# Six ring slots, leftovers loaded ahead by ScalarE, and the mask added on TensorE in a segment-recurrent attention kernel

## The chip, the cores and the metric

The kernel runs on one core of a Trainium2 chip. The metric is device time in microseconds of one execution. Four runs of the kernel before gave a median of 2346.21 us (2343.95 to 2352.86); the profiled execution took 2343.33 us.

## The reference

Two attentions run over 2048 rows of width 640, and their outputs are put side by side. The first, A, is a sliding, dilated attention with 32 heads of 20. The second, B, is a recurrence, and most of the time lies there:

```python
for s in range(64):                                  # 2048 rows in segments of 32
    h = concat([mem, x[32*s : 32*s+32]])             # 8 memory rows + 32 rows = 40
    q, k, v = h @ Wq, h @ Wk, h @ Wv                 # 32 heads of 192: 640 -> 6144, each
    p = softmax(where(mask, q @ k.T * scale, -1e9))  # 40 x 40 per head
    o = (p @ v) @ Wo                                 # 6144 -> 640
    mem, out = o[:8], o[8:]
```

The memory of a segment is the first 8 rows of the output of the one before, so the segments cannot be done side by side. The mask lets every row see the memory, memory rows see all, and the others see what is not later than themselves.

## The kernel before, in words

**Part A** (0 to 236 us of the span) computes the first attention; `between` (line 404) slips work for B into it. **The left phase** (236 to 461 us) does ahead, for all segments at once, what does not depend on the memory: of the 32 rows of a segment the last 8, the "leftovers", have their queries, keys and values computed and put into HBM (`qk_scr`, `v_scr`). The other 24 rows go with the 8 memory rows as one block of 32 columns through **the segment loop** (461 to 2262 us, 64 iterations). **The tail** (2262 to 2341 us) multiplies the leftovers' results, which the loop has put into `ol_scr`, by Wo for all segments.

One iteration projects the 32 columns with twelve weight groups, Q0, K0, Q1, K1 to Q3, K3 and V0 to V3, each of 8 heads (`proj`, line 583: 20 matmuls of 128x32 by 384 columns, four side by side). ACT copies the Q results and DVE the K results to bf16 in one of three buffers `abc0` to `abc2` (`keep_`, line 598), PE transposes Q and K of a group (`turn`), ACT and DVE copy the turned heads into `XL` (`turned_out`, line 616). `scores(0)` uses groups 0 and 1, `scores(1)` groups 2 and 3; the softmax of each half runs on DVE and ACT in three pieces (`softmax_1` to `softmax_3`); `turn_p` transposes the probabilities, `pv` multiplies by V, `heads_out` and `left_out` copy the results, and sixteen output units (`o_units`, 12 matmuls each) sum Wo's part into one bank. Two DVE steps then make the next segment's input `HT` from it.

**The weights.** They do not all fit in SBUF. Of every projection group the heads of j = 0, 1, 2 stay resident, and the unit of j = 3 (128 rows of 1,920 bf16, 480 KB) is streamed in each iteration; so are four of the sixteen output units, 16 streamed units in all. They take turns in five ring slots (four in `temp`, one in `ring4`). `SLOT` (line 365) says which unit sits where, and `done` (line 571) issues, on SyncE, the load of the unit that follows in a slot as soon as the matmuls that used the slot are through:

```python
SLOT = [0, 1, 2, 3, 0, 4, 1, 2, 0, 3, 4, 1, 0, 2, 3, 4]  # Q0 K0 Q1 K1 Q2 K2 Q3 K3 V0 V1 V2 V3 and four output units
```

**The order.** Each engine runs its own list in the order in which lines 747 to 808 call. `SegmentLoop.analyse` (line 240) works out the semaphore waits from named resources that an operation reads and writes. An operation can name resources as `also`: it waits for their readers, and counts as a reader of them itself. DMAs are operations of the engine that issues them, and a wait ahead of one holds everything behind it on that engine. SyncE's list holds the weight loads, the leftovers' queries and keys (`load_left`, line 623, two in an iteration), their values (`load_vl`) and four loads of the next segment's rows (line 755). `load_left` puts queries and keys side by side over memory that `OT` and `PT` share, and POOL copies the queries into place (line 625). ACT's list holds, beside its copies, the store of the leftovers' results (line 801) and of the output rows (line 808).

## Time and profile before

| what | value |
|---|---|
| median of 4 runs | 2346.21 us |
| profiled execution | 2343.33 us, its span 2341.2 us |
| busy in the span | PE 75%, weight loads on PE 48%, DVE 41%, ACT 30%, POOL 2% |
| granted TensorE clock | 0.943 |
| HBM read, written | 573.62 MB, 39.62 MB |
| DMA engines | 261 GB/s over the span |

In the profile a row of a group has line, engine, operation, out<-in, shapes and count, then busy us and mean ns of one, then idle us of the engine just before and what ended that. A row of a wait has who waited for whom: total us, times, longest us. A row of the order in time has start us, us, engine, line, operation, and in brackets the idle time before it. "SPq" and "ACTq" are the DMA issues of SyncE and ACT. The DMA share is the mean over the core's 16 DMA engines.

### The profile page before, as it was taken

What the parts mean: (1) busy time and instruction counts of PE and PEld (TensorE: products, weight loads), DVE (VectorE), ACT (ScalarE), POOL (GpSimd) and SP (SyncE); (2) the same over time, 40 slices, a digit from 0 to 9 for tenths busy, and PEclk for the clock granted to TensorE, in tenths of its full rate; (3) what the DMA queues carried; (4) which work ended last, traced back from release to release, by engine and by line L of the source; (5) the groups of instructions that cost most, each with busy time, mean ns of one, the idle gap of its engine ahead of it and who ended that gap; (6) DMA issues with size and microseconds to landing.
All of it is one profiled execution on the core that took longest, in us unless ns stands there. A gap on an engine that the chain in (4) does not pass through costs nothing.

```text
span 2341.2 us, 108094 instructions
## 1 busy us (share of the span) xinstructions
PE 1765.8 (75%) x45924; PEld 1113.1 (48%) x45948; DVE 961.2 (41%) x2284; ACT 691.8 (30%) x1633; POOL 50.5 (2%) x150
## 2 busy tenths in 40 slices
PE   7796958777777777777787777777777777777749
PEld 5442423355445554554455545454454444444436
DVE  3575312244444444444444444444444444444430
ACT  4342312123323333222332333222222323222221
POOL 0000000000000000000000000000000000000000
PEclk9898979799999999899999999999989999999989
DMA  8030975789888888888998889888888888888881
GB/s 225 22 105 20 188 225 178 230 281 317 297 291 307 301 304 302 288 291 292 311 305 293 299 296 310 292 292 304 301 283 290 292 289 301 286 293 284 287 311 62
DMA packets 259558, 611.24 MB, mean 261 GB/s; under 512 B 90608, under 2 KB 120432, under 8 KB 256768
## 3 DMA queue, kind: packets, MB, share of 16 engines
q1 hardware_dynamic: 223872, 591.35, 75.7%
q10 hardware_dynamic: 35648, 19.34, 2.8%
q8 instruction: 29, 0.48, 0.1%
q14 instruction: 9, 0.07, 0.0%
HBM read 573.62 MB, written 39.62 MB: 262 GB/s over the span
## 4 chain that ended last, share of the span: by engine, by line
issue 76%; PE 12%; DMA 6%; DVE 2%; ACT 1%; POOL 1%; POOLq 0%; ACTq 0%; SPq 0%; DVEq 0%
PE pq L75 3%; PE ps L444 3%; PE yp L836 2%; DMA v_scr<-abc 2%; DMA temp<-in_B_Wk_dram 1%; DMA ws<-temp 1%; DVE pv L157 1%; PE po L87 1%; PE ps L458 1%; POOL XL L625 1%; PE oT L162 1%; DMA temp<-in_B_Wo_dram 1%; DMA v_scr<-ring 1%; PE L L108 1%; PE pp L141 0%
## 5 line engine op out<-in xcount | busy, mean ns | idle before, releaser
L592 PE MATMUL bank<-temp,XL 128*32 128x384 bf16 x3200 | 641.8, 339 | 0.0
L592 PE MATMUL bank<-w,XL 128*32 128x384 bf16 x7680 | 530.2, 346 | 62.8 <-DMA temp<-ws 62.4
L592 PE MATMUL bank<-wq,XL 128*32 128x384 bf16 x3840 | 265.6, 339 | 217.7 <-DMA temp<-ws 201.2
L600 ACT CAST abc<-bank 128x384 bf16<-128x384 f32 x512 | 240.3, 479 | 577.3 <-PE bank L592 571.5
L592 PEld LDWEIGHTS bank<-w,XL 128*32 128x32 bf16 x7680 | 243.6, 100 | 233.6 <-DMA temp<-ws 85.7
L592 PEld LDWEIGHTS bank<-temp,XL 128*32 128x32 bf16 x3200 | 279.3, 99 | 0.0
L592 PEld LDWEIGHTS bank<-wq,XL 128*32 128x32 bf16 x3840 | 114.0, 98 | 323.1 <-DMA temp<-ws 262.1
L618 DVE COPY XL<-bank 128x384 bf16<-128x384 bf16 x256 | 90.9, 355 | 353.5 <-PE bank L612 203.3
L739 PE MATMUL bank<-w,XL 128*32 128x160 bf16 x9216 | 231.5, 236 | 1.5 <-issue 1.5
L600 DVE CAST abc<-bank 128x384 bf16<-128x384 f32 x256 | 141.6, 553 | 205.0 <-PE bank L592 204.9
L651 PE MATMUL bank<-XL 128*64 128x40 bf16 (+1 forms) x4096 | 123.2, 189 | 110.4 <-POOL XL L625 110.3
L739 PEld LDWEIGHTS bank<-w,XL 128*32 128x32 bf16 x9216 | 173.5, 98 | 19.8 <-issue 3.7
L618 ACT COPY XL<-bank 128x384 bf16<-128x384 bf16 x256 | 122.7, 479 | 191.9 <-PE bank L612 109.2
L651 PEld LDWEIGHTS bank<-XL 128*64 128x64 bf16 (+1 forms) x4096 | 106.1, 112 | 151.5 <-POOL XL L625 144.9
L721 ACT CAST XL<-bank 128x192 bf16<-128x192 f32 x256 | 81.7, 319 | 232.0 <-PE bank L714 155.2
L721 DVE CAST XL<-bank 128x192 bf16<-128x192 f32 x256 | 91.0, 355 | 138.7 <-ACT XL L721 138.6
L592 PE MATMUL bank<-ring,XL 128*32 128x384 bf16 x640 | 145.6, 365 | 0.0
L612 PE MATMUL bank<-ident,abc 128*128 128x128 bf16 x1536 | 136.3, 227 | 0.1
L612 PEld LDWEIGHTS bank<-ident,abc 128*128 128x128 bf16 x1536 | 90.6, 101 | 86.9 <-issue 45.7
L662 DVE SCALAR_TENSOR_TENSOR t<-bank,XL 128x320 f32<-128x320 f32 x128 | 62.9, 492 | 122.9 <-PE bank L651 122.9
L625 POOL COPY XL<-XL 128x192 bf16<-128x192 bf16 x128 | 44.7, 349 | 1752.1 <-DMA XL<-qk_scr 1752.1
L688 PE MATMUL bank<-ident,t 128*128 128x128 bf16 x256 | 36.7, 225 | 55.5 <-DVE t L679 55.5
(111 smaller groups left out, 2039.8 us busy)
## 6 DMA issues: line engine op xcount, KB each, us to landing
temp<-ws SPq DMA_DIRECT2D x644, 480.0 KB, 5.1
temp<-in_B_Wo_dram SPq DMA_DIRECT2D x196, 480.0 KB, 5.3
ring<-ws SPq DMA_DIRECT2D x129, 480.0 KB, 6.1
ring<-in_B_Wo_dram SPq DMA_DIRECT2D x64, 480.0 KB, 3.4
qk_scr<-st SPq DMA_DIRECT2D x2, 6144.0 KB, 17.3
XL<-qk_scr SPq DMA_DIRECT2D x128, 96.0 KB, 4.3
abc<-v_scr SPq DMA_DIRECT2D x64, 96.0 KB, 4.3
ol_scr<-XL ACTq DMA_DIRECT2D x64, 96.0 KB, 6.7
```

The source lines that it names most:

```text
L75: nc.tensor.matmul(pq[32 * dd:32 * dd + 32, :], lhsT=w[:, 4 * c + dd, :], rhs=xT[:, dc, :], start=(dc == 0), stop=(dc == 4), tile_position ...
L444: nc.tensor.matmul(ps[:], lhsT=w[:, dc, o:o + 128], rhs=XL[:, dc], start=(dc == 0), stop=(dc == 4))
L592: i = MM(ps[32 * j:32 * j + 32, :], lhsT=HT[:, dc, :], rhs=ws[j][:, dc, :], start=(dc == 0), stop=(dc == 4), tile_position=(0, 32 * j))
L600: op(e, [f"b{b}"], [f"abc{k}"], lambda s: COPY[e](ABC[k], bank[b][:, 0:384]))
L612: i = nc.tensor.transpose(tp[ty][:, c], ABC[nat[ty, r]][:, 128 * c:128 * c + 128], ident)
L618: op(e, [("b3", "b5")[ty]], [QPARTS[ty][h]], lambda s: COPY[e](QT[:, 12 * h:12 * h + 12, 0:32] if ty == Q else KT[:, 12 * h:12 * h + 12, 0:4],
L625: op("POOL", ["PT", "PTL"], ["Q.l"], lambda s: nc.gpsimd.tensor_copy(QT[:, :, 32:L], ql))
L651: i = MM(Sps[64 * e:64 * e + 64, 4 * rr + j, :], lhsT=XLb[lo:hi, L * (4 * cc + j):L * (4 * cc + j) + 64], rhs=KT[lo:hi, 4 * cc + j], start ...
L662: op("DVE", [f"b{SB[t]}"], ["t1"], lambda s: V_.scalar_tensor_tensor(out=t1[:], in0=Sps, scalar=scale, in1=mask.unsqueeze(1).to_broadcast( ...
L721: op(e, [f"b{4 + j}"], [f"OT{t}.{j}"], lambda s: COPY[e](OT[t][:, 6 * j:6 * j + 6], ots[j].rearrange("p r x l -> p (r x) l")[:, :, 0:32]), ...
L739: i = MM(Y[32 * g:32 * g + 32], lhsT=OT[t][:, 6 * j + 3 * rr + x], rhs=w[:, x, 160 * g:160 * g + 160], start=(t == 0 and n == 0 and x == 0 ...
L836: nc.tensor.matmul(yp[h][:], lhsT=OL[tb][:, 24 * (r // 2) + 6 * j + 3 * (r % 2) + x].rearrange("p s l -> p (s l)"), rhs=w[:, x, 320 * h:32 ...
```

## The change

- **Ring.** Six slots and 17 streamed units: output units (1,0), (0,3), (2,0), (2,2), (3,3) are streamed instead of (0,2), (0,3), (2,1), (2,3), so 11 output units stay resident instead of 12. `SLOT` is new. The tail loads five units instead of four.
- **Queues.** SyncE's list in the loop holds weight loads only. The leftovers' keys, queries, values and the next rows are loaded by ACT. Keys and queries are loaded separately; those of half 0 are loaded in the iteration before, through one more row of `qk_scr`. The next rows come as one load of 128 rows, for which `x_scr` has another layout, with zeros where the memory rows stand; it is written by 12 transfers in part A.
- **Waits.** An operation that names a resource as `also` no longer waits for others that do; only a writer waits for both. The results of the two halves lie elsewhere (`OT`, `OL`), and the leftovers' store is split in two.
- **Softmax.** The mask, divided by the scale, is added in PSUM by two matmuls with the identity ahead of each score block; the scale is applied in the exponential. The DVE pass that scaled and masked is gone, and the next two read PSUM.
- **Order.** Q3 is copied after turn 2 and into another buffer; five output units (not three) stand ahead of the second `turn_p`, and three (not two) behind it; none of the first half stands behind the second `pv`.
- **Rows in HBM.** The streamed units' scratch has rows of 2,048 elements of which 1,920 are used.

SyncE's list at the start of an iteration of the kernel before; `ws_0_2_3` is Q's (0) group 2, unit j = 3, `ws_1` is K's, `ws_2` V's:

```order
L575 DMA temp_88<-ws_0_2_3_72 128x1920
L575 DMA temp_88<-ws_0_3_3_74 128x1920
L575 DMA temp_88<-ws_1_3_3_75 128x1920
L624 DMA XL_89<-qk_scr_81 128x2x192
L575 DMA temp_88<-ws_2_1_3_77 128x1920
L756 DMA z_3577<-x_scr_80 24x160
L575 DMA temp_88<-ws_2_0_3_76 128x1920
```

The row of z stands four times there. The same place in the changed kernel, issued after Q0, K0, Q1, K1, Q2 and K2 have used their slots:

```order
L584 DMA temp_87<-ws_0_3_3_73 128x1920
L584 DMA temp_87<-ws_2_0_3_75 128x1920
L584 DMA temp_87<-ws_1_3_3_74 128x1920
L584 DMA temp_87<-ws_2_1_3_76 128x1920
L584 DMA ring4_3587<-ws_2_2_3_77 128x1920
L584 DMA ring5_3588<-in_B_Wo_dram 128x1920
```

Q0's slot now takes Q3's unit and not Q2's, and nothing but weights is left in the list.

ACT's list before, from the first copy of turned probabilities to the exponential of the second half (a register row is the count of a wait):

```order
L692 COPY XL<-bank_4000 128x160
L325 REGISTER_ALU
L721 CAST XL<-bank_4001 128x192
L325 REGISTER_ALU
L721 CAST XL<-bank_4001 128x192
L670 ACTIVATE t_2613<-t_2613 128x320
```

The same place in the changed kernel, from the load of the next rows on:

```order
L796 DMA z<-x_scr 128x160
L330 REGISTER_ALU
L705 COPY XL<-bank_4010 128x160
L330 REGISTER_ALU
L734 CAST XL<-bank_4011 128x192 x2
L330 REGISTER_ALU
L683 ACTIVATE t_2624<-t_2624 128x320
```

The two copies of heads follow each other without a wait between, and a DMA issue has come ahead of them.

ACT's list before, at the end of an iteration:

```order
L692 COPY XL<-bank_4000 128x160
L721 CAST XL<-bank_4001 128x192
L801 DMA ol_scr<-XL 128x2x192
L807 ACTIVATE z<-bank_3999,bdf 128x160
L808 DMA out_dram<-z 4x32x160
```

And in the changed kernel, from the copy of V3 on:

```order
L609 CAST abc_2622<-bank_4008 128x384
L743 DMA ol_scr<-XL 128x192
L633 DMA XL<-qk_scr 128x192
L705 COPY XL<-bank_4010 128x160
L734 CAST XL<-bank_4011 128x192 x2
L636 DMA XL<-qk_scr 128x192
L743 DMA ol_scr<-t_2624 128x192
L825 CAST z<-bank_4009 128x160
L826 DMA out_dram<-z 4x32x160
```

The first store (L743) and the loads of the next iteration's keys (L633) and queries (L636) now stand among the copies.

The diff, cut to its core:

```diff
-                for k in rd + also:
+                for k in rd:
                     readers.setdefault(k, []).append(me)
+                for k in also:
+                    takers.setdefault(k, []).append(me)
...
-    N_STR, N_RING = 16, 5
-    SLOT = [0, 1, 2, 3, 0, 4, 1, 2, 0, 3, 4, 1, 0, 2, 3, 4]
+    N_STR, N_RING = 17, 6
+    SLOT = [0, 1, 2, 3, 4, 5, 0, 2, 1, 3, 4, 0, 1, 2, 3, 4, 5]
...
-    ws_scr = {u: dram.tile([128, US], BF16, name=f"ws_{u[0]}_{u[1]}_{u[2]}") for u in streamed if u[0] != O}
+    ws_scr = {u: dram.tile([128, 2048], BF16, name=f"ws_{u[0]}_{u[1]}_{u[2]}")[:, 0:US] for u in streamed if u[0] != O}
...
-    OT = [XLb[:, KO * t:KO * t + 4 * PW].rearrange("p (a l) -> p a l", l=32) for t in range(2)]
-    OL = XLb[:, 0:2 * KO].rearrange("p (t n) -> p t n", t=2)[:, :, 4 * PW:5 * PW]
+    OT = [XLb[:, o:o + 4 * PW].rearrange("p (a l) -> p a l", l=32) for o in (KO, 0)]
+    OL = [XLb[:, 4 * PW:KO], t1b[:, 256:256 + PW]]
...
-    def load_left(t):
-        op("SP", [], ["K.l", "PT", "PTL"], lambda s: nc.sync.dma_start(left, qk_scr[:, :, t, s, :]), dma="qkl")
-        op("POOL", ["PT", "PTL"], ["Q.l"], lambda s: nc.gpsimd.tensor_copy(QT[:, :, 32:L], ql))
+    def load_kl(t, ahead):
+        op("ACT", [], ["K.l"], lambda s: nc.scalar.dma_start(kl, qk_scr[:, 0, t, s + ahead, :]), dma="kl")
+    def load_ql(t, ahead):
+        op("ACT", [], ["PT", "PTL"], lambda s: nc.scalar.dma_start(ql, qk_scr[:, 1, t, s + ahead, :]), dma="ql")
+    def place_ql():
+        op("POOL", ["PT", "PTL"], ["Q.l", "Q.e"], lambda s: nc.gpsimd.tensor_copy(QT[:, :, 32:L], ql.rearrange("p (a k) -> p a k", k=NL)))
     def load_vl():
-        op("SP", [], ["abc2"], lambda s: nc.sync.dma_start(ABC[2], v_scr[s]), dma="vl")
+        op("ACT", [], ["abc2"], lambda s: nc.scalar.dma_start(ABC[2], v_scr[s]), dma="vl")
...
+            for e in range(2):
+                h = slice(64 * e, 64 * e + 64)
+                MM(Sps[h], lhsT=ident[h, h], rhs=mask[h].unsqueeze(1).to_broadcast([64, 8, L]), start=True, stop=False,
+                   tile_position=(64 * e, 64 * e), skip_group_check=True)
...
-        op("DVE", [f"b{SB[t]}"], ["t1"], lambda s: V_.scalar_tensor_tensor(
-            out=t1[:], in0=Sps, scalar=scale, in1=mask.unsqueeze(1).to_broadcast([128, 8, L]),
-            op0=ALU.mult, op1=ALU.add))
-        op("DVE", ["t1"], ["mx"], lambda s: V_.tensor_reduce(out=mx, in_=t1[:], axis=AX.X, op=ALU.max))
+        op("DVE", [f"b{SB[t]}"], ["mx"], lambda s: V_.tensor_reduce(out=mx, in_=Sps, axis=AX.X, op=ALU.max))
...
-    load_left(0)
     turn(0)
...
     qk(K, 1)
-    for g in range(4):
-        op("SP", [], [ZG[g]], lambda s, g=g: nc.sync.dma_start(
-            z[32 * g:32 * g + NX, :], x_scr[s + 1, 0:NX, 160 * g:160 * g + 160]), dma="xz")
+    load_ql(1, 0)
...
+    load_vl()
     qk(K, 2)
     scores(0)
+    load_kl(1, 0)
+    place_ql()
     softmax_1(0)
-    qk(Q, 3)
-    load_left(1)
+    proj(Q, 3)
     turn(2)
+    keep_("ACT", Q, 3)
...
+    store_left(0)
+    load_kl(0, 1)
     softmax_3(1)
-    o_units(0, 0, 3)
+    o_units(0, 0, 5)
     turn_p(1)
-    o_units(0, 3, 5)
+    o_units(0, 5, 8)
     pv(1)
...
-    o_units(0, 5, 8)
+    load_ql(0, 1)
+    store_left(1)
     o_units(1, 0, 8)
```

More of the change, by code (lines that the diff above doesn't have):

```diff
@@ L268, in analyse @@
                         want(ev, True)
+                    if k in wr:
+                        for ev in takers.get(k, []):
+                            want(ev, True)
                     if k in writer:
@@ L362, in part_b @@
         order += [(O, 2 * t + rr, j) for j in range(4) for rr in range(2)]
-    streamed = [u for u in order if u[0] != O and u[2] == 3 or u in ((O, 0, 2), (O, 0, 3), (O, 2, 1), (O, 2, 3))]
-    N_STR, N_RING = 16, 5
-    SLOT = [0, 1, 2, 3, 0, 4, 1, 2, 0, 3, 4, 1, 0, 2, 3, 4]
+    streamed = [u for u in order if u[0] != O and u[2] == 3 or u in ((O, 1, 0), (O, 0, 3), (O, 2, 0), (O, 2, 2), (O, 3, 3))]
+    N_STR, N_RING = 17, 6
+    SLOT = [0, 1, 2, 3, 4, 5, 0, 2, 1, 3, 4, 0, 1, 2, 3, 4, 5]
     assert len(streamed) == N_STR
@@ L502, in part_b @@
     psum = lctx.enter_context(tc.tile_pool(name="b_ps", bufs=1, space=PSUM))
-    rows, toks = bdf[:, 3:4], bdf[:, 4:5]
+    rows = bdf[:, 3:4]
     XLb = XL[:].rearrange("p c s l -> p (c s l)")
@@ L742, in emit @@
                 return i
[L743 removed]
+            op("PE", [f"OT{t}.{j}", wkey(u)] + OPARTS[t], ["b2"], emit)
             done([u])
[L746 removed]
     qk(Q, 0)
+    place_ql()
     qk(K, 0)
     qk(Q, 1)
[L750 removed]
     turn(0)
@@ L780, in part_b @@
     keep_("ACT", V, 1)
+    op("ACT", [], ["z"], lambda s: nc.scalar.dma_start(z[:], x_scr[s + 1]), dma="xz")
     turn_p(0)
```

89 lines of the change are left out of this document (45 added, 44 removed).

## The prediction

> **What bounds the kernel now.** I read the page first, then stretches by stage, the waits, the queue of SyncE, and one iteration in order of time. The page gives the span; the stretches are part A, the left phase, the segment loop and the tail.
>
> ```profile
> span 2341.2 us, 108094 instructions
> ...
> 0.00:236.00 236.00, 183.27 (x1870) 99.50 (x1885) 133.58 (x99) 86.27 (x152) 4.34 (x14) 0.91 0.34 92
> 236.00:461.00 225.00, 168.94 (x793) 81.77 (x800) 57.51 (x129) 50.63 (x129) 1.44 (x8) 0.87 0.74 208
> 461.00:2262.00 1801.00, 1359.18 (x42880) 893.58 (x42880) 764.53 (x2048) 542.25 (x1344) 44.70 (x128) 0.96 0.87 296
> 2262.00:2341.00 79.00, 54.43 (x384) 38.26 (x384) 5.62 (x8) 12.63 (x9) 0.00 (x0) 0.87 0.34 129
> ```
>
> After the stretch come busy PE, weight loads, DVE, ACT and POOL, the granted clock, the DMA share and GB/s. The loop is 77% of the span. No engine fills it: PE is busy 75%, and the 16 DMA engines 87%, at 296 GB/s. The unit that K2 needs in slot 4 is issued once before the loop and once at each iteration's end, so SyncE's first and last such issue stand 64 iterations apart:
>
> ```profile
> 461.34 0.32 SPq L313 DMA_DIRECT2D ring<-ws  x1
> ...
> 2260.61 0.32 SPq L575 DMA_DIRECT2D ring<-ws  x1
> ```
>
> (2260.61 - 461.34) / 64 = 28.1 us for an iteration. What PE waits for in it, over the whole run (total, times, longest):
>
> ```profile
> PE bank L592 <- DMA temp<-ws: 263.6, 215, 2.6
> ...
> PE bank L651 <- POOL XL L625: 110.3, 109, 2.9
> ...
> PE bank L688 <- DVE t L679: 55.5, 48, 1.2
> ```
>
> By 64, that is 4.1 us for streamed weights, 1.7 us of the two score blocks for POOL's copy of the leftover queries, and 0.9 us of the turning of the probabilities for the softmax. Without them an iteration is 28.1 - 4.1 - 1.7 - 0.9 = 21.4 us of PE work and short joints.
>
> The weight waits are strange with DMA engines that are 13% idle. SyncE's waits and one iteration show why:
>
> ```profile
> SPq L624 <- DMA ol_scr<-XL: 87.1, 60, 2.8
> ...
> SPq L756 <- DMA out_dram<-z: 37.3, 21, 3.0
> ```
>
> ```profile
> 1272.40 1.95 SPq L575 DMA_DIRECT2D temp<-ws  x3
> 1276.54 0.59 SPq L624 DMA_DIRECT2D XL<-qk_scr  x1
> 1277.26 0.50 SPq L575 DMA_DIRECT2D temp<-ws  x1
> 1279.79 1.84 SPq L756 DMA_DIRECT2D z<-x_scr  x4
> 1281.74 0.35 SPq L575 DMA_DIRECT2D temp<-ws  x1
> ```
>
> ```profile
> 1277.69 0.34 PE L592 MATMUL bank<-wq,XL 128*32 128x384 bf16 x3 [1.84 <-DMA temp<-ws]
> ...
> 1285.39 0.34 PE L592 MATMUL bank<-w,XL 128*32 128x384 bf16 x3 [1.19 <-DMA temp<-ws]
> ```
>
> SyncE takes its issues in program order. The leftover load at 1276.54 stood until the store of the last iteration's leftovers had landed, and the four loads of z at 1279.79 held it 1.84 us more. Q2's matmuls began at 1277.69, but the load that their slot had to take next, V0's, went out at 1281.74, and V0 started late at 1285.39. Q2's own load could go out only when Q0 had freed slot 0, at 1272.40: five slots give it three units' notice.
>
> **The change part by part.**
>
> *Queue order.* SyncE keeps only weights: qkl (two), vl and the four z loads leave it, so each weight load goes out as its slot falls free. I price this at nothing by itself; it lets the DMA queue run full.
>
> *Ring.* Six slots instead of five, 17 units instead of 16. Q2 and K2 are now loaded in the iteration before, so the largest wait loses its cause. The cost is one more unit. Bytes over the loop, by queue (packets, MB, share):
>
> ```profile
> q1 hardware_dynamic: 200522, 523.65, 85.0%
> q10 hardware_dynamic: 25452, 8.78, 1.8%
> ```
>
> (523.65 + 8.78) / 64 = 8.32 MB an iteration. One unit is 480 KB = 0.49 MB, z goes from 30 to 40 KB: 8.82 MB. The price is a rate. Mean GB/s by mean share is 296 / 0.87 = 340 at full share. In stretches where the queue never runs dry:
>
> ```profile
> 1272.40:1280.40 8.00, 5.38 (x112) 2.81 (x104) 2.02 (x5) 2.34 (x5) 0.00 (x0) 1.00 0.99 364
> 1328.70:1336.70 8.00, 5.73 (x100) 2.97 (x92) 1.46 (x4) 2.00 (x5) 0.00 (x0) 0.84 1.00 355
> 1356.00:1364.00 8.00, 5.93 (x132) 3.28 (x120) 1.83 (x4) 2.34 (x5) 0.00 (x0) 1.00 1.01 369
> ```
>
> So a full queue needs 8.82 / 0.369 = 23.9 us to 8.82 / 0.340 = 25.9 us. I take 25.5 us (346 GB/s), nearer the mean, since the fast stretches hold few of the small packets. The Trainium skill ("DMA: Bandwidth & Descriptors", "Where 436 GB/s comes from") puts the memory side of such loads at about 358 GB/s for a core; an estimate by it is 24.6 us an iteration, 2122 us in all. The trace agrees: 355 to 369.
>
> *Leftover queries and keys.* They are loaded ahead, by ACT: part 0 in the iteration before, part 1 as soon as the first scores have been read. POOL's copy no longer ends the wait: 1.7 us goes, and what is next late is the copy of turned heads, at most about 0.3 us off. Each load is on ACT's queue, in front of copies that PE needs; of before the nearest rows are ACT's own issues:
>
> ```profile
> 1269.43 0.39 ACTq L801 DMA_DIRECT2D ol_scr<-XL  x1
> ...
> 1270.81 0.39 ACT L807 ACTIVATE z<-bank,bdf 128x160 bf16<-128x160 f32 x1 [2.22 <-DVE XL L806]
> 1271.38 0.57 ACTq L808 DMA_DIRECT2D out_dram<-z  x1
> ```
>
> ACT issues 9 where it issued 2: seven more at 0.39 to 0.57 us, 3.4 us an iteration, beside 542.25 / 64 = 8.5 us of work: half full. Three (ql, vl, kl) stand before copies that PE wants; if all three showed, 1.5 us.
>
> *Softmax and scores.* The scale-and-mask pass on DVE goes, and the two next passes read PSUM. The rows of the removed pass and of the next, and the wait between copies of the heads that goes:
>
> ```profile
> L662 DVE SCALAR_TENSOR_TENSOR t<-bank,XL 128x320 f32<-128x320 f32 x128 | 62.9, 492 | 122.9 <-PE bank L651 122.9
> L665 DVE TENSOR_REDUCE XL<-t 128x8 f32<-128x320 f32 x128 | 62.2, 486 | 4.4
> ```
>
> ```profile
> DVE XL L721 <- ACT XL L721: 138.6, 192, 1.4
> ```
>
> 0.49 us leaves each chain; the two engines' copies no longer alternate (138.6 / 128 blocks = 1.1 us of DVE's waiting a block, of which I count half); and two more output units stand ahead of the turning (36 matmuls take 0.80 us below, so 24 some 0.5). Together that covers the 0.9 us.
>
> ```profile
> 1267.82 0.80 PE L739 MATMUL bank<-w,XL 128*32 128x160 bf16 x36
> ```
>  Added on PE: two mask matmuls a block, four an iteration. Nearest are the tail's 320-wide ones, on the chain that ended last; before them stands the load that they waited for:
>
> ```profile
> 2269.40 18.66 DMA temp<-in_B_Wo_dram
> ...
> 2288.10 49.07 PE yp L836 x360
> ```
>
> 49.07 / 360 = 0.14 us each back to back: 0.3 us if the pairs run side by side, at most 0.6. I take 0.3. Reading PSUM instead of SBUF: the removed pass read PSUM in 492 ns, the next one the same size from SBUF in 486, so zero.
>
> *Given back on PE.* The two kinds of copy on ACT:
>
> ```profile
> L600 ACT CAST abc<-bank 128x384 bf16<-128x384 f32 x512 | 240.3, 479 | 577.3 <-PE bank L592 571.5
> ...
> L721 ACT CAST XL<-bank 128x192 bf16<-128x192 f32 x256 | 81.7, 319 | 232.0 <-PE bank L714 155.2 <-DVE XL L721 76.8
> ```
>
> Q3 is copied after turn 2, so ACT has one more copy (479 ns) before K3's can be turned: 0 to 0.48 us, I take 0.3. Three units no longer stand behind the second product of probabilities, so the first unit after it waits for its copy: 319 ns, some 0.5 us with the passing of signals (0.3 to 1).
>
> PE's side is then 21.4 + 0.3 + 0.3 + 0.5 = 22.5 us, below the queue's 25.5. The queue sets the iteration, and about 3 us of weight waits stay in it, spread otherwise.
>
> *Outside the loop.* x_scr is written by 12 small transfers instead of 2, while the DMA engines are 34% busy; the scheduler also orders part A anew. One unit's load leaves the left phase. In the tail PE begins at 2282.45 and does four units' 24 matmuls before it needs a streamed one:
>
> ```profile
> 2282.45 5.37 PE L836 MATMUL yp<-w,w 128*128 128x320 bf16 x24 [21.68 <-ACT w L829]
> ```
>
> The first streamed unit lands at 2269.40 + 18.66 = 2288.06. Now the second unit of the order is streamed, so 18 of those 24 come after that: 18 x 0.14 = 2.5 us later. For the rest I take zero, with 8 us either way.
>
> The sum: 64 x (28.1 - 25.5) = 166 us less, 2.5 more. The profiled execution took 2343.3 us (span 2341.2), 2.9 below the median of the four runs, 2346.2. 2343.3 - 166 + 2.5 = **2180 us**. With 24.2 to 26.6 us an iteration the case's own range is 2095 to 2250.
>
> **The rivals.**
>
> *PE sets the loop.* If a queue that never empties runs faster still, PE's 22.5 us decides: 2343.3 + 2.5 - 64 x 5.6 = 1987 us. It needs 392 GB/s. For it, one stretch of 2 us:
>
> ```profile
> 1289.00:1291.00 2.00, 1.97 (x116) 1.77 (x120) 1.19 (x3) 0.55 (x2) 0.00 (x0) 1.00 1.05 426
> ```
>
> Against it: no stretch of 8 us passes 369. The Trainium skill ("HBM Reference", "Specifications") has a core streaming alone at about 425 GB/s; by that PE would decide, and only the 2 us stretch agrees. Chance 0.10.
>
> *ACT's queue becomes a wait.* Its three exposed issues, 1.5 us, add to 25.5 where a late copy frees slots late: 27.0 us, 2275 us. For it: ACT also holds wait points in order, so kl waits for the scores while copies stand behind. Against it: PE has 3 us in hand. Chance 0.13.
>
> *The waits only move.* The ring deepens, but the added unit eats the gain: 28.0 us, 2339 us. Against it is the idle 13%. Chance 0.05.
>
> *The scratch rows slow the queue: slower.* Their pitch goes from 3,840 to 4,096 bytes, so each row starts at the same place of a 4 KB block. The queue is even at 28.1 us, 8.82 / 28.1 = 314 GB/s; if the five output units stay at 346 (7.1 us for 2.46 MB), with 0.46 MB of small ones (1.3 us), the twelve scratch units must take 19.7 us, 1.64 each instead of 1.42. Priced at the lowest that the loop shows over long stretches, 296 GB/s for all, 29.8 us: 2455 us. The trace has no such pitch; for it speaks only that weights are two thirds scratch. The Trainium skill ("DMA: Bandwidth & Descriptors", "Latency and other measured facts") warns of large power-of-two pitches, but its pitches begin at 512 KiB; no run here shows 4 KiB. Chance 0.09.
>
> **How the numbers follow.** The forecast has 0.63. A measurement of this kernel tells about 0.3% (7 us) from no change. Faster: 0.63 + 0.10 + 0.13 and 0.02 of the moved waits, 0.88; within it 0.03; slower 0.09. Leaving out the two far cases (0.10 and 0.09), the range takes the forecast's own and ACT's, with the 8 us: 2090 to 2300.
>
> **What would show it.** Right: the DMA row at 9 in every slice of the loop, 335 to 365 GB/s, an iteration of 24 to 26.6 us, no POOL wait before the scores, PE still waiting 150 to 250 us for weights, at K3, Q2 and the first output units rather than at Q2 and V0. Wrong: a DMA share below 0.95 with PE waiting for ACT or DVE, or a full share at 320 GB/s or less.

## The result, and the profile after

The changed kernel takes **2090.65 us** (median of 10 runs, 2082.91 to 2094.36); the kernel before took 2343.95 us beside it (15 runs, 2327.48 to 2356.64). The ratio is 0.8916, 95% interval 0.8895 to 0.8938. That is faster, and 89 us below the 2180 us forecast; the stated range began at 2090. The profiled execution took 2090.02 us, its span 2088.1.

The stretches of the changed kernel, cut at the same four places as those of before (part A, left phase, loop, tail; after the stretch busy PE, weight loads, DVE, ACT, POOL, then granted clock, DMA share, GB/s):

```profile
0.00:236.00 236.00, 178.06 (x1849) 103.00 (x1860) 134.02 (x98) 84.08 (x147) 5.45 (x15) 0.91 0.36 91
236.00:467.50 231.50, 169.15 (x816) 82.16 (x824) 57.35 (x129) 52.78 (x134) 1.21 (x7) 0.89 0.73 204
467.50:2004.50 1537.00, 1344.52 (x43136) 898.83 (x43136) 700.37 (x1918) 525.91 (x1343) 44.88 (x128) 0.99 0.99 367
2004.50:2088.00 83.50, 54.62 (x384) 38.33 (x384) 6.35 (x10) 12.81 (x9) 0.00 (x0) 0.86 0.36 139
```

The loop's DMA share went from 0.87 to 0.99, its rate from 296 to 367 GB/s. The load for K2's slot, by which the iteration was measured before, is again issued once ahead of the loop and last at its end (the second of the two in the second row, 2003.88 + 0.94 - 0.32 = 2004.50):

```profile
467.54 0.43 SPq L318 DMA_DIRECT2D ring<-ws  x1
...
2003.88 0.94 SPq L584 DMA_DIRECT2D ring<-ws  x2
```

(2004.50 - 467.54) / 64 = 24.0 us an iteration, where the forecast had 25.5 and before had 28.1. The loop gave 64 x 4.1 = 262 us; what lies outside it grew from 2341.2 - 64 x 28.11 = 541.9 us to 2088.1 - 64 x 24.02 = 551.1 us (28.11 and 24.02 before rounding).

What PE and its weight loader wait for in the loop of the changed kernel:

```profile
PEld bank L601 <- DMA temp<-ws: 78.7, 157, 1.6
...
PE bank L601 <- DVE XL L824: 62.5, 61, 1.0
PEld bank L664 <- DMA XL<-qk_scr: 60.4, 64, 1.6
PE bank L664 <- DMA XL<-qk_scr: 49.3, 64, 1.5
...
PEld bank L601 <- DMA ring<-ws: 36.6, 62, 1.0
PE bank L755 <- ACT XL L734: 32.4, 63, 0.5
PE bank L601 <- DMA temp<-ws: 28.2, 85, 1.4
...
PE bank L601 <- DMA ring<-ws: 12.1, 55, 0.6
```

PE's 263.6 us for weights of before are 28.2 and 12.1 now, with 78.7 and 36.6 on the weight loader. POOL is gone from PE's list. A new row stands there: the second score block waits for the leftover keys of half 1 (49.3 us, once in each iteration). SyncE in the loop waits only for PE to free a slot:

```profile
SPq L584 <- PE bank L601: 787.2, 704, 4.9
SPq L584 <- PE bank L755: 200.8, 273, 3.6
...
SPq L584 <- PE bank L703: 76.8, 64, 1.3
```

One iteration of the changed kernel in two parts, and SyncE's loads around the cut:

```profile
1050.00:1066.00 16.00, 14.65 (x383) 8.96 (x379) 7.47 (x19) 5.92 (x15) 0.70 (x2) 1.00 1.02 399
1066.00:1073.00 7.00, 5.71 (x295) 4.63 (x283) 3.42 (x12) 2.04 (x6) 0.00 (x0) 1.00 0.95 317
```

```profile
1060.30 2.51 SPq L584 DMA_DIRECT2D temp<-in_B_Wo_dram  x3
1066.24 0.33 SPq L584 DMA_DIRECT2D ring<-in_B_Wo_dram  x1
```

The iteration isn't uniform. In its first 16 us, ten projections free slots quickly and the queue moves 399 GB/s. From the last load of the first row (1060.30 + 2.51 - 0.33 = 1062.48) to 1066.24 no slot comes free, because PE is at probabilities, scores and values, and the queue thins out to 317 GB/s at a share that still reads 0.95.

### The profile page after: what moved, and what is told of

It reads as the page before. It is cut to its first block, busy times and chain, and to the rows that moved or that the text cites. A ratio compares the mean times of both kernels' runs of the same rounds, so it can differ in the third digit from the quotient of the medians.

```text
span 2088.1 us, 108557 instructions
## 1 busy us (share of the span) xinstructions
PE 1746.4 (84%) x46184; PEld 1122.3 (54%) x46204; DVE 898.1 (43%) x2155; ACT 675.6 (32%) x1633; POOL 51.5 (2%) x150
## 4 chain that ended last, share of the span: by engine, by line
PE 46%; DMA 45%; issue 3%; DVE 3%; ACT 2%; ACTq 1%; SPq 0%; DVEq 0%
DMA XL<-qk_scr 15%; DMA ring<-ws 15%; PE bank L601 12%; PE bank L755 9%; DMA temp<-ws 5%; PE bank L668 5%; DMA temp<-in_B_Wo_dram 4%; PE pq L75 3%; PE bank L722 3%; PE yp L855 3%; PE ps L452 2%; DMA v_scr<-abc 2%; DMA w<-in_B_Wv_dram 2%; PE bank L664 1%; DVE pv L157 1%
## 5 line engine op out<-in xcount | busy, mean ns | idle before, releaser
L601 PE MATMUL bank<-temp,XL 128*32 128x384 bf16 x2880 | 549.7, 331 | 0.0
L601 PE MATMUL bank<-w,XL 128*32 128x384 bf16 x7680 | 498.8, 334 | 23.0 <-DMA temp<-ws 21.1
L601 PEld LDWEIGHTS bank<-w,XL 128*32 128x32 bf16 x7680 | 241.0, 98 | 173.5 <-DMA temp<-ws 43.4
L601 PEld LDWEIGHTS bank<-temp,XL 128*32 128x32 bf16 x2880 | 251.7, 97 | 0.0
L755 PE MATMUL bank<-w,XL 128*32 128x160 bf16 x8448 | 217.0, 235 | 1.6 <-issue 1.6
L601 PE MATMUL bank<-ring,XL 128*32 128x384 bf16 x960 | 195.5, 336 | 0.0
L755 PEld LDWEIGHTS bank<-w,XL 128*32 128x32 bf16 x8448 | 162.9, 98 | 17.2 <-issue 3.0
L734 ACT CAST XL<-bank 128x192 bf16<-128x192 f32 x256 | 69.2, 322 | 203.7 <-PE bank L727 203.7
L621 PEld LDWEIGHTS bank<-ident,abc 128*128 128x128 bf16 x1536 | 86.7, 98 | 81.8 <-issue 25.5
L678 DVE TENSOR_REDUCE XL<-bank 128x8 f32<-128x320 f32 x128 | 62.9, 492 | 146.5 <-PE bank L668 146.5
L755 PE MATMUL bank<-temp,XL 128*32 128x160 bf16 x2304 | 74.7, 236 | 35.7 <-ACT XL L734 32.4
L686 DVE TENSOR_REDUCE XL<-t 128x8 f32<-128x320 f32 x128 | 61.4, 480 | 57.8 <-ACT t L683 57.8
```

What stands on the lines that cost most here:

```text
L601: i = MM(ps[32 * j:32 * j + 32, :], lhsT=HT[:, dc, :], rhs=ws[j][:, dc, :], start=(dc == 0), stop=(dc == 4), tile_position=(0, 32 * j))
L621: i = nc.tensor.transpose(tp[ty][:, c], ABC[nat[ty, r]][:, 128 * c:128 * c + 128], ident)
L678: op("DVE", [f"b{SB[t]}"], ["mx"], lambda s: V_.tensor_reduce(out=mx, in_=Sps, axis=AX.X, op=ALU.max))
L686: op("DVE", ["t1"], ["sm"], lambda s: V_.tensor_reduce(out=sm, in_=t1[:], axis=AX.X, op=ALU.add))
L734: op(e, [f"b{4 + j}"], [f"OT{t}.{j}"], lambda s: COPY[e](OT[t][:, 6 * j:6 * j + 6], ots[j].rearrange("p r x l -> p (r x) l")[:, :, 0:32]), ...
L755: i = MM(Y[32 * g:32 * g + 32], lhsT=OT[t][:, 6 * j + 3 * rr + x], rhs=w[:, x, 160 * g:160 * g + 160], start=(t == 0 and n == 0 and x == 0 ...
```

## The experiments

All kernels carry one edit of the loop's bookkeeping: its registers start 4,096 higher, and a spare semaphore is raised behind the waits of POOL and of the score blocks. **The control** is the changed kernel with that alone.

> Control for all the kernels below that come from the changed kernel: the changed kernel itself, with the loop's register bookkeeping offset by a constant and one spare semaphore increment behind the waits of POOL and of the two score blocks. Both theories: 2080 to 2100 us, as the changed kernel (2090.65); anything over 0.5% away would be the price of that bookkeeping and is to be taken off the others.

Measured: 2092.3 us, ratio to the kernel before 0.8932 (0.8887 to 0.8977). The bookkeeping costs nothing that shows; the others are compared with this. The two kernels made from the one before have no such control of their own.

The window from 600 to 1900 us inside the loop serves below for all. The control:

```profile
600.00:1900.00 1300.00, 1130.70 (x36511) 756.24 (x36510) 595.33 (x1626) 444.70 (x1137) 38.41 (x109) 0.99 0.99 369
```

### Bytes and slots

**Seven slots.**

```
-    ... (O, 2, 0), (O, 2, 2), (O, 3, 3))]
-    N_STR, N_RING = 17, 6
-    SLOT = [0, 1, 2, 3, 4, 5, 0, 2, 1, 3, 4, 0, 1, 2, 3, 4, 5]
+    ... (O, 2, 0), (O, 2, 1), (O, 2, 2), (O, 3, 3))]
+    N_STR, N_RING = 18, 7
+    SLOT = [0, 1, 2, 3, 4, 5, 6, 0, 1, 2, 3, 0, 1, 2, 3, 4, 5, 6]
```

> One more output unit is streamed instead of resident, its 3,840 bytes a partition become a seventh slot: 0.49 MB more an iteration, and more notice for every unit. Theory 'the full queue sets the iteration' (8.82 MB in 23.9 us, 369 GB/s): 9.31 / 0.369 = 25.2 us, 64 x 1.3 = 85 us more, 2175 us. Theory 'PE's own list sets it, with its joints, and the queue only keeps up': the list is unchanged, 2080 to 2105 us, and the queue then shows more than 369 GB/s (up to 9.31 / 23.9 = 390).

Measured: 2193.88 us, ratio 0.9368 (0.9313 to 0.9423): 102 us more, where "queue" had 85 and "PE's own list" next to nothing. But PE doesn't wait longer for weights: the rows `temp<-ws` and `ring<-ws` fall from 35.9 and 12.8 us in the control to 15.8 and 9.6. What grows is the second score block's wait for the leftover keys of half 1, from the control's

```profile
PE bank L667 <- DMA XL<-qk_scr: 55.8, 64, 1.4
```

to

```profile
PE bank L667 <- DMA XL<-qk_scr: 89.8, 64, 1.9
```

and the granted clock is 0.95 instead of 0.99:

```profile
600.00:1900.00 1300.00, 1114.23 (x34195) 735.33 (x34187) 557.63 (x1526) 411.35 (x1068) 37.86 (x102) 0.95 0.98 365
```

Where the clock was full, an iteration takes 24.7 us here (23 of 56) and 23.8 in the control (52 of 56); in the mean it takes 1.5 us more, so that the slower clock goes with some 0.6 of them. The run shows that the added load costs time. That it costs it as a full queue's time is not shown.

**Five slots, as before.** The old three lines (16, 5, the old `SLOT`) in the changed kernel.

> The ring of before (5 slots, 16 units, 8.33 MB) under all the other edits. Theory 'queue': 8.33 / 0.369 = 22.6 us would be possible, 2005 us, if no unit comes late. Theory 'PE's list': no gain from fewer bytes, and with five slots Q2 and K2 get their weights in the same iteration again, so part of Q2's wait of before (1.9 us of the 28.1) comes back: 0.5 to 1.9 us an iteration, 2120 to 2210 us. In 'queue' the ring itself gave no gain; in 'PE's list' it gave that much.

Measured: 2145.83 us, ratio 0.9171 (0.9125 to 0.9217): 54 us more, with 6% fewer bytes. "Queue" falls, and the time lies in the range of "PE's list": PE waits for weights again, 214.9 us where the control has 48.7, nearly half of it ahead of Q2.

```profile
PE bank L604 <- DMA temp<-ws: 214.9, 138, 3.1
```

```profile
600.00:1900.00 1300.00, 1095.73 (x35305) 734.05 (x35295) 575.71 (x1575) 428.02 (x1103) 36.79 (x106) 0.99 0.96 337
```

The share is 0.96, but the rate 337 GB/s. With fewer loads in flight (3.4 on average, 4.2 in the changed kernel; the table below) the DMA engines read as busy all the same, and move less.

**Five slots, dealt out by time.**

```
-    SLOT = [0, 1, 2, 3, 0, 4, 1, 2, 0, 3, 4, 1, 0, 2, 3, 4]
+    SLOT = [0, 1, 2, 3, 4, 0, 1, 3, 2, 4, 0, 3, 1, 2, 4, 3]
```

> Five slots and 16 units (8.33 MB) again, as in the run with the old ring, but the slots are dealt out by time: the slot that is used four times serves K1, K3, V3 and the last output unit, and Q2 and K2 no longer take the slots that Q0 frees first, so the shortest notice between a slot's release and its next use is 4.5 us of PE's list instead of 3.2. Theory 'the full queue sets the iteration, if no unit comes late': 8.33 / 0.369 = 22.6 us, with some lateness 22.8 to 23.6 us, 2020 to 2070 us, below the changed kernel. Rival 'five slots are too few to fill the queue, however dealt': 337 GB/s as with the old deal, 24.4 to 24.8 us, 2125 to 2150 us.

Measured: 2113.91 us, ratio 0.9049 (0.9011 to 0.9087), between the two theories. Of the 54 us that six slots gave over five, the deal alone is worth 32.

```profile
600.00:1900.00 1300.00, 1106.97 (x35876) 748.46 (x35866) 585.29 (x1599) 439.09 (x1119) 37.19 (x107) 1.00 0.97 342
```

**Half of every streamed load**, in the changed kernel and in the one before:

```
-nc.sync.dma_start(ws_ring[slot(u)], source(streamed[k]))
+nc.sync.dma_start(ws_ring[slot(u)][:, 0:960], source(streamed[k])[:, 0:960])
```

> Each streamed unit's load in the loop brings only the first half of every row, so half of the streamed weights are left out and the iteration moves 4.6 MB instead of 8.82. The time left is that of PE's list with its joints. Theory 'queue': the list is well below 23.9 us; with the 22.5 us of the prediction's sum 2090 - 64 x 1.4 = 2000 us. Theory 'PE's list': at least 23.4 us an iteration, 2060 to 2090 us. In between, both end within half a microsecond of each other.

Measured: 1956.92 us, ratio 0.8364 (0.8321 to 0.8407). Q0 starts every 21.85 us, nearly all iterations within 0.01 us of it: this is PE's list, and nothing is ever late. The side of "queue" is right, 43 us below its 2000, and PE's list is even shorter than the 22.5 us of the prediction.

> The kernel before, each streamed unit's load in the loop bringing only the first half of every row; half of the streamed weights are left out. Theory 'the weight waits of before are lateness of bytes': the 4.1 us go, 24.0 us an iteration, 2080 us, and a little less if the small loads land sooner. Rival 'they are SyncE's order': V0's load still goes out after the loads of z and Q2's after Q0, 25 to 26 us, 2145 to 2210 us.

Measured: 2045.21 us, ratio 0.873 (0.8697 to 0.8762), below both, and nearer the first. The mean distance of Q0's starts is 23.4 us. So lateness of loads cost the kernel before 28.1 - 23.4 = 4.7 us an iteration, and the changed one 24.0 - 21.85 = 2.15; the list itself became 1.55 us shorter. (With half the bytes the small loads land sooner as well, so "lateness" holds theirs too.) Of the 2.15 us, PE's rows in the changed kernel name 1.4: 0.6 for weights (28.2 and 12.1 us over 64 iterations) and 0.8 for the leftover keys of half 1 (49.3 us). With half the bytes PE waits for no load in the loop.

### The parts of the change

**The small loads on SyncE's queue again** (`nc.scalar` to `nc.sync` for kl, ql, vl and z).

> The changed kernel with its seven small loads (kl, ql, vl, z) issued by SyncE again, at the same places of the program. Known by now: PE's list alone takes 21.85 us an iteration, and seven slots cost the queue's time for the added bytes. Theory 'the queue runs full only because SyncE keeps nothing but weights': SyncE stands at the waits of the small loads, the queue gets holes, share under 0.97, 24.4 to 25.4 us an iteration, 2120 to 2190 us. Rival 'six slots give notice enough, whoever issues': 2080 to 2100 us, share still 0.99.

Measured: 2087.25 us, ratio 0.8939 (0.8872 to 0.9007): no change. The rival was right; with six slots it doesn't matter who issues them.

```profile
600.00:1900.00 1300.00, 1140.26 (x36641) 761.57 (x36645) 595.71 (x1634) 441.65 (x1143) 37.84 (x109) 0.99 1.00 370
```

**Scratch rows end to end** (`dram.tile([128, 2048], ...)[:, 0:US]` back to `dram.tile([128, US], ...)`).

> The changed kernel with its scratch rows end to end again (3,840 bytes) instead of 4,096 apart. Theory 'full queue, and its rate doesn't depend on the pitch': 2080 to 2100 us. Rival 'the pitch made the rate': the queue falls back towards 346 GB/s, 25.5 us, 2190 us. Rival 'the pitch slows the queue, as one of the prediction's rivals had it': the time falls, to 2030 us if the rate gains 4%.

Measured: 2091.57 us, ratio 0.8945 (0.8876 to 0.9013). The pitch bears on nothing here.

**`also` counted as reading**, as before.

> The changed kernel, with the operations that only take part of a buffer ('also') counted as readers again, as before: the two engines' copies of heads wait for each other. Theory 'queue': PE's list grows from 21.85 by at most 1 us and stays below the queue's 23.9, so nothing moves: 2080 to 2100 us. Rival 'waits of PE and of the queue add up': 0.5 to 1.0 us an iteration, 2120 to 2155 us.

Measured: 2110.6 us, ratio 0.9034 (0.8967 to 0.9102): 18 us more, 0.3 us an iteration, between the two.

**The leftovers loaded late.** Both halves' keys and queries are loaded behind Q1 and behind Q3's matmuls, as before, and nothing in the iteration ahead.

```
     qk(Q, 1)
+    load_kl(0, 0)
+    load_ql(0, 0)
+    place_ql()
...
     proj(Q, 3)
+    load_kl(1, 0)
+    load_ql(1, 0)
+    place_ql()
```

> The changed kernel with both parts' leftover keys and queries loaded as late as before (part 0 behind Q1, part 1 behind Q3's matmuls), on ACT's queue. Theory 'queue' with PE's 2 us in hand: PE waits for POOL's copy again (1.7 us an iteration in the kernel before), most of that is hidden, 2085 to 2120 us. Rival 'a wait of PE adds to the iteration, because it also frees weights later': 1 to 2 us an iteration, 2150 to 2220 us.

Measured: 2533.63 us, ratio 1.0864 (1.0806 to 1.0922): 441 us more, 6.9 us an iteration, and slower than the kernel before. Both theories were far too low.

```profile
PEld bank L667 <- issue: 414.2, 64, 7.8
PE bank L667 <- ACT XL L630: 391.3, 64, 7.4
```

```profile
600.00:1900.00 1300.00, 957.12 (x28308) 628.53 (x28308) 461.18 (x1260) 348.33 (x882) 29.15 (x84) 0.88 0.81 286
```

The first score block waits 6.1 us each time for ACT's copy of the turned queries. In the changed kernel that copy must follow POOL's copy of the leftover queries (both write the strip `Q.e`), and POOL waits for the load. So this is the cost of late leftovers in the new order of writing, where a late load also stops ACT; in the old order it cost 1.7 us. The loads themselves land sooner than in the control, 4.5 us after issue against 5.8.

**Six slots alone**, in the kernel before.

> The kernel before with six slots and 17 units, nothing else. Theory 'the ring is most of it': Q2's wait of 1.9 us goes, 26.2 us or less an iteration, 2220 us or less. Rival 'the edits only work together' (SyncE still stands at the small loads, PE still waits for POOL and for the softmax, and 0.49 MB more are to be moved): 27.2 us or more, 2290 to 2360 us.

Measured: 2463.24 us, ratio 1.0536 (1.0488 to 1.0583): the ring alone makes the kernel before 5% slower. Its waits, SyncE's own among them:

```profile
DVE XL L621 <- DMA ol_scr<-XL: 243.8, 62, 5.2
...
PE bank L654 <- POOL XL L628: 194.3, 111, 3.2
...
PE bank L595 <- DMA temp<-ws: 29.6, 43, 1.7
...
PE bank L595 <- DMA ring<-ws: 16.3, 44, 1.0
```

```profile
SPq L627 <- DMA ol_scr<-XL: 168.9, 62, 3.4
```

DVE's row in the kernel before was

```profile
DVE XL L618 <- DMA ol_scr<-XL: 150.2, 61, 3.6
```

One iteration in stretches:

```profile
1001.00:1009.00 8.00, 6.09 (x132) 3.51 (x132) 1.74 (x4) 2.53 (x6) 0.00 (x0) 1.00 0.98 357
1009.00:1011.70 2.70, 0.26 (x8) 0.00 (x0) 0.56 (x1) 0.00 (x0) 0.35 (x1) 1.00 0.82 273
1011.70:1016.00 4.30, 4.20 (x70) 2.47 (x74) 1.83 (x4) 1.22 (x3) 0.00 (x0) 0.61 0.49 141
1016.00:1022.00 6.00, 3.90 (x98) 2.41 (x91) 2.39 (x7) 1.84 (x5) 0.35 (x1) 1.00 1.00 361
```

The ring does what it was to do: PE's 263.6 us for weights are 29.6 and 16.3. But the last iteration's store of leftovers takes 7.8 us to land, where it took 6.7 in the kernel before. The row of DMA issues with six slots, then that of the kernel before:

```profile
ol_scr<-XL ACTq DMA_DIRECT2D x64, 96.0 KB, 7.8
```

```profile
ol_scr<-XL ACTq DMA_DIRECT2D x64, 96.0 KB, 6.7
```

The leftover loads don't land later (4.0 us, and 4.3 before). SyncE, holding the leftover load, stands at that store 168.9 us instead of 87.1; DVE's copies of turned keys stand at it too; POOL's copy comes late, and in this iteration PE stops for 2.54 us ahead of the scores:

```profile
1008.93 0.33 PE L595 MATMUL bank<-ring,XL 128*32 128x384 bf16 x1
1011.80 0.94 PE L654 MATMUL bank<-XL 128*64 128x40 bf16 x32 [2.54 <-POOL XL L628]
...
1012.97 0.53 PE L595 MATMUL bank<-wq,XL 128*32 128x384 bf16 x3
```

Then comes a second price: for 4.3 us after the stop the granted clock is 0.61, and a projection's matmuls take 0.53 us instead of 0.33. From 1007.91 to 1013.09 SyncE issues no weight load, and the queue falls to 141 GB/s. Such stops recur: 33 of 2 to 3 us between 600 and 1900 us, with a mean clock of 0.55 in the 4 us behind them (0.94 behind the 124 stops of 1 to 1.5 us).

**The softmax of before** (scale and mask in a DVE pass, no mask matmuls):

```
-                MM(Sps[h], lhsT=ident[h, h], rhs=mask[h].unsqueeze(1)..., start=True, stop=False, ...)
...
+        op("DVE", [f"b{SB[t]}"], ["t1"], lambda s: V_.scalar_tensor_tensor(
+            out=t1[:], in0=Sps, scalar=scale, in1=mask.unsqueeze(1)..., op0=ALU.mult, op1=ALU.add))
```

> The changed kernel with the softmax of before: scale and mask in a pass of DVE (492 ns), no mask matmuls. Theory 'queue' with PE's 2 us in hand: 2080 to 2105 us. Rival 'the shorter chain was needed': PE waits 0.5 us more at each turning of the probabilities, 1.0 us an iteration, 2140 to 2160 us.

Measured: **2064.56 us**, ratio 0.8817 (0.8782 to 0.8853), against 0.8932 (0.8887 to 0.8977) of the control: faster by 1.3%. This part of the change costs some 28 us. Neither theory had it.

```profile
600.00:1900.00 1300.00, 1124.16 (x36989) 765.13 (x36988) 657.86 (x1771) 457.12 (x1162) 39.36 (x111) 0.99 1.01 376
```

### PE's joints, and what the rate hangs on

**Leftover keys of half 1 early, and two output units moved.**

```
-    load_kl(1, 0)
+    place_kl1()        # POOL, from a place of its own, loaded ahead of Q2
...
-    o_units(0, 0, 5)
+    o_units(0, 0, 4)
     turn_p(1)
-    o_units(0, 5, 8)
+    o_units(0, 4, 6)
     pv(1)
...
+    o_units(0, 6, 8)
     o_units(1, 0, 8)
```

> PE's two longest joints go: the leftover keys of part 1 are loaded early into a place of their own and put in place by POOL (PE waits 0.8 us for that load), and two output units move behind the second product of probabilities, in front of the unit that waits for copied heads (0.6 us). Theory 'queue': PE already has 2 us in hand, nothing moves: 2080 to 2100 us, and PE waits as much longer for weights. Rival 'PE's joints add to the queue's time': 0.7 to 1.4 us an iteration less, 2000 to 2045 us.

Measured: 2143.85 us, ratio 0.9175 (0.9099 to 0.9252): slower, which neither expected. The early keys lie over the softmax's sums, and that made a wait of its own, 2.7 us each time:

```profile
DVE XL L698 <- POOL XL L645: 168.7, 63, 3.8
```

So this run doesn't tell the theories apart. Its second edit alone:

> Of the run with two edits only the second: four output units ahead of turning the probabilities instead of five, two instead of three behind it, and two in front of the units that wait for copied heads. It is meant to tell what made that run slower. If the moved units did (their weights come free later): 2110 to 2145 us. If the leftover keys' new place did (the softmax's sums now wait for POOL's copy, 168.7 us in all in its trace): 2080 to 2100 us, since PE has 2 us an iteration in hand.

Measured: 2084.8 us, ratio 0.893 (0.8882 to 0.8978): no change. The keys' new place made the other run slow.

**The moved units and SyncE's small loads together.**

> The two edits of the changed kernel that came out at or just below its time, together: two output units moved ahead of the wait for copied heads, and the small loads issued by SyncE. Theory 'queue': neither moves bytes, 2070 to 2095 us. Rival 'PE's joints still count a little': 2050 to 2070 us.

Measured: 2095.62 us, ratio 0.894 (0.8906 to 0.8974): no change either.

**Two thirds of the output matmuls left out.**

```
-                for x in range(3):
+                for x in range(1):
```

> The changed kernel with two thirds of the output projection's matmuls left out in the loop (one of each unit's three row blocks), all loads as they were: PE's list falls from 21.85 to about 19.7 us (128 of 192 groups, 3.2 us x 2/3). Theory 'the full queue alone sets the iteration': 2080 to 2100 us, 368 to 375 GB/s. Rival 'PE and queue share it, since a late PE frees slots late': about half of the 2.1 us shows, 2010 to 2045 us, and the queue then moves 385 GB/s or more.

Measured: 2087.0 us, ratio 0.8916 (0.8878 to 0.8954), as "queue" says. But the row takes back part of what that shows:

```profile
600.00:1900.00 1300.00, 1132.32 (x29760) 683.23 (x29757) 597.47 (x1639) 445.96 (x1146) 37.84 (x109) 0.88 1.00 370
```

The granted clock is 0.88, not 0.99. Behind the thinned-out output units the next three projections take 1.1 to 1.2 us from first to last matmul instead of 0.67 (means of the trace's iterations), so some 1.5 of the 2.1 us left out came back, and PE's list was cut by little.

**V2's projection moved** ahead of the second score block, into the stretch in which no slot comes free; in the control's kernel and in the one with the softmax of before:

```
     turn_p(0)
+    proj(V, 2)
     scores(1)
...
     left_out(0)
-    proj(V, 2)
     keep_("ACT", V, 2)
```

> The changed kernel with V2's projection moved ahead of the second block of scores, so that its slot is freed about 2.5 us sooner; bytes, copies and slots as they were. Theory 'depth': 369 GB/s is no ceiling but a mean of some 405 GB/s with five or more weight loads in flight and some 300 with three, and between V1's and V2's release (13.0 to 17.0 us of the iteration) no load goes out, so the queue thins out; with the hole closed in part the mean is 375 to 385 GB/s, 22.9 to 23.5 us, 2030 to 2065 us. Rival 'ceiling': 369 GB/s is what such loads give, and the order doesn't matter: 2080 to 2100 us.

Measured: 2083.37 us, ratio 0.891 (0.8869 to 0.8951): a trifle, not told from none.

> The same move in the kernel with the softmax of before, which came out at 2064.6 us. Theory 'depth': 0.3 to 0.8 us an iteration less, 2010 to 2045 us. Rival 'ceiling, and the 26 us were something else': 2055 to 2075 us.

Measured: 2080.97 us, ratio 0.8905 (0.8872 to 0.8939): 16 us slower than without the move. The move brought waits of its own: ahead of V2, which needs the bank that V1's copy empties, PE now stands 0.60 us, and ahead of V3, whose bank the softmax reads, 0.69 us (from the last matmul's start to the next's; 0.15 where nothing waits).

To see whether the rate has a ceiling, the bytes of the DMA packets between 600 and 1900 us were sorted by how many streamed loads were under way, from issue to landing (counted 1.9 us ahead of the packet, since bytes trail the issue; with no such shift the changed kernel's row reads 294, 333, 363, 397, 393). GB/s, and the share of the time in brackets:

```
loads under way      2           3           4           5           6        mean
kernel before    230 (26%)   314 (45%)   350 (22%)   384  (3%)                2.9
five slots       252  (8%)   338 (50%)   353 (40%)   359  (2%)                3.4
changed kernel   233  (5%)   310 (18%)   378 (31%)   402 (43%)   406  (4%)    4.2
softmax of bef.  245  (3%)   328 (20%)   381 (34%)   401 (41%)   407  (2%)    4.2
seven slots      244  (7%)   302 (18%)   354 (11%)   395 (23%)   405 (37%)    4.7
```

In each kernel the rate grows with the count. In the three with six or seven slots it is 395 to 407 GB/s with five or six loads; some 400 is called the ceiling below. The count alone doesn't give it, for with five slots five loads under way moved 359 (2% of the time). The changed kernel has five or six under way for 47% of its time. And where it isn't is a matter of place. The iterations of two kernels, each cut into twelve equal parts, GB/s (means):

```
changed kernel   343  409  412  410  404  397  404  406  288  280  328  355
V2 moved         330  362  393  409  405  395  405  406  389  231  385  337
```

The changed kernel runs at the ceiling for seven parts of twelve and falls short from V2 through the output units to the next Q0. Its mean of 367 is a mixture. With V2 moved the low place moves by a part, and stays.

## Where the prediction was right, and the step that failed

**The failed step is the rate of a full queue.** That loads would go on bounding the iteration, above PE's list, came true. The time that they need did not: "So a full queue needs 23.9 to 25.9 us ... I take 25.5 us (346 GB/s), nearer the mean, since the fast stretches hold few of the small packets." It needed 24.0: 8.82 MB at 367 GB/s. 64 x 1.5 = 96 us lie in this term; the rest of the sum missed by 6.7 us the other way (2180 - 96 + 6.7 = 2091). The forecast's own range, 24.2 to 26.6 us or 2095 to 2250, did not hold either; only the 8 us allowed outside the loop bring it to 2090. The mean of before, 296 / 0.87 = 340, was taken as the rate of a full queue. But the share hardly tells rates apart: at 0.96 to 1.01 the runs show 337, 342, 365, 369 and 376 GB/s. The mean of before also held much time with few loads (26% with two, 5% in the changed kernel). The rows of 355 to 369 GB/s that were quoted were the better guide, and they were not the ceiling either; nor is it so that no stretch of 8 us passed 369, for the best one in the loop of before has 388. The Trainium skill ("DMA: Bandwidth & Descriptors", "Where 436 GB/s comes from") has some 358 GB/s for a core from memory; here the measurements decide, with 367 over the loop and 399 over 16 us.

Nor are the 24.0 us a full queue's time. At 402 GB/s, the changed kernel's rate with five loads under way, 8.82 MB would take 21.9 us (an estimate), as long as PE's list of 21.85. So "The queue sets the iteration" holds only in part: loads and PE need about the same, and the rest is each waiting for the other, PE for weights and leftover keys, the queue for slots while PE is at probabilities and values. That fits the runs in which the same bytes take another time: 28 us less with the softmax of before, 18 us more with `also` as before. A queue that sets the iteration alone would give neither.

**PE's side.** 22.5 us were forecast, 21.85 measured with half the bytes. The list fell by 1.55 us, where (28.1 - 4.1) - 22.5 = 1.5 were forecast. But of the 2.15 us of lateness only 0.6 is PE waiting for weights, where "about 3 us of weight waits" were to stay: 40 us on PE (28.2, and 12.1 for loads into `ring`), counted as the 263.6 of before, and not 150 to 250. They are longest at K3 and Q2, as forecast, and almost none are at the output units. The first unit behind the second product waits 0.5 us for its copy (32.4 us, 63 times), as priced.

**Queue order,** priced at nothing by itself: with six slots it is worth nothing with the rest either. The prediction's reading that SyncE's order starved the queue of before has no run of its own; with half the bytes and the old order hardly a weight is late (23.4 us).

**The ring.** That Q2's wait goes was right in the main: 0.4 us is left of 1.9. "The cost is one more unit" was not the whole cost. Small transfers that others wait for can land later: in the kernel before the store of leftovers (6.7 to 7.8 us), and six slots alone are 5% slower there; in the changed kernel the leftover loads (5.4, 5.8 and 6.0 us with five, six and seven slots), and PE waits for the keys from six slots on. Under the other edits six slots give 54 us, 32 of which a better deal of five would give too.

**Leftovers ahead.** "1.7 us goes": it went, and a wait for the keys of half 1 came (49.3 us on PE, 0.8 us an iteration), more than the "at most about 0.3 us" of what is next late. And 1.7 us is what the wait cost in the old order of writing; in the new one late loading costs 6.9 us. Six slots add 126 us to the kernel before (2463.24 against 2336.78 beside it) and take 54 from the changed one, so the ring's worth depends on the other edits, while the prediction added its terms up. That the early leftovers are the edit that turns it is likely, and not shown by a run of its own.

**Softmax and scores.** The term was booked as covering the turning's wait at 0.3 us of PE time; the trace has 0.5 (twice 0.25). The wait did go, but with the softmax of before the kernel is 28 us faster, 0.43 us an iteration: five output units ahead of the turning cover the old chain as well. Why it gains that much isn't settled. In the trace of the changed kernel the score matmuls start 0.25 us behind the mask matmuls, twice in an iteration, and the second time in the stretch that is short of loads, where PE's time delays the next slot. That would account for it, and from V1's last matmul to V2's first, the stretch with the second block, the old softmax takes 2.84 us instead of 3.31; but the DVE pass also gives the bank of scores free sooner, and no run separates the two.

**Outside the loop.** 9.2 us more, where 2.5 with 8 either way were forecast: 6.2 ahead of the loop, 3.0 in the tail. In the tail PE stops at the second unit, the first streamed one, as forecast:

```profile
2025.09 1.78 PE L855 MATMUL yp<-w,w 128*128 128x320 bf16 x6 [20.62 <-ACT w L848]
...
2030.72 1.76 PE L855 MATMUL yp<-temp,w 128*128 128x320 bf16 x6 [3.85 <-DMA temp<-in_B_Wo_dram]
```

**The rivals.** PE setting the loop fell: with half the bytes the same list runs 135 us faster. But its condition, a queue above 392 GB/s, was met in seven parts of twelve. ACT's queue as a wait fell: moving its loads to SyncE changes nothing. The scratch rows' pitch fell. That the waits only move fell for the whole change, and is what six slots alone do, at a loss. The fastest kernel is the changed one with the softmax of before, 2064.56 us.

What stays open: whether the iteration can be freed of its low stretch. The run that cut PE's work lost its cut to the clock, and the run that moved V2 made new waits, so it wasn't shown that 400 GB/s can be had throughout. The wait for the leftover keys of half 1 is open too, as the run that loaded them early made a wait of its own.

## What to carry to other kernels

Don't divide the mean rate by the mean DMA share to get the rate of a full queue; look for stretches with many loads under way, and for those in which no buffer comes free. When a ring gets deeper, look who waits for the small loads and stores that share the queue; they can land later, and what the ring takes from one wait can come back in theirs (48.7 to 25.4 us for weights, 55.8 to 89.8 for keys, from six slots to seven). Try the parts of a compound change one by one once it is in: here one part took back 28 us of a gain that is 253.

## What the runs showed of the hardware

- A stop of PE of 2.5 us is followed by 4.3 us at a granted clock of 0.61 (six slots alone), in which a projection's 128x384 matmuls take 0.53 us instead of 0.33; behind the 33 stops of 2 to 3 us in that trace the mean is 0.55 over 4 us. The Trainium skill ("TensorE: Matmul & The Clock Gate", "HAM oscillation — how this bites in real kernels") warns of idle gaps of over some 3.4 us; here the clock fell behind stops of 2 to 3 us, in stretches that hold shorter stops too. Thinned-out matmuls went with it as well: with two thirds of the output matmuls left out the clock is 0.88, with only five stops of 2 us or more in 1300 us.
- The DMA share saturates before the rate does: 0.96 at 337 GB/s, 0.98 at 365, 1.01 at 376, and 1.02 at 399 within an iteration.
- Loads of 480 KB in rows of 3,840 bytes reach some 400 GB/s on this one core with five under way (six or seven slots), and 405 to 407 with six. With five, six and seven slots a load into `temp` lands 5.4, 6.1 and 6.8 us after its issue, so the added slots go mostly into longer waiting in the queue.
